# Decay attention, then a max-gated MLP, on one core: a planner with other costs and slack, and unsplit float32 products with the values in the second batch

## The chip, the core and the metric

The kernel runs on one core of a Trainium2 chip as a single program. The metric is the device time in microseconds (us) of one execution. The kernel before has a median of 991.08 us over 3 runs (990.32 to 992.14).

## The reference, cut to what matters

There are 8 batches of 8 heads, with 576 positions and 64 features per head. Everything is float32, except that the four weight matrices arrive as float64.

```python
scores = q @ k.T / 8                       # (8, 8, 576, 576)
cum = cumsum(log(clip(f, 1e-4, 1)))        # decay, per head
scores = where(causal, -1e9, scores + cum[:, None] - cum[None, :])
attn = exp(scores - rowmax); attn /= attn.sum(-1) + 1e-9
x = (attn @ v)  ->  (4608, 512)            # heads side by side
h = max(x @ w1, x @ w2, x @ w3)            # (4608, 768)
out = h @ w_out                            # (4608, 512)
```

## The kernel before, in words

**Halved operands.** Where TensorE (PE) is to work at its quick float32r format, an operand X is split into a rounded half Xh and a remainder Xl, and a product is taken as Xh·Y_h + Xh·Y_l + Xl·Y_h, three matmuls into one PSUM bank. ScalarE (ACT) writes the rounded half and VectorE (DVE) subtracts to get the remainder. The first batch (8 heads, `n < H * NB32`) isn't split: its scores and its products with the values are plain float32 matmuls, one instruction for each block.

**The attention of one head** is done as keys on the partitions and queries along the columns, in two units: unit 1 has queries 256 to 575 (five key blocks, 1,216 columns in all), unit 2 has queries 0 to 255 (two blocks, 384 columns). In the first batch unit 1 is cut into "a" and "b". `scores` (L577) makes these steps for each unit:

- a first pass on PE (`pass_a`, L606) into the score banks `s`, and the causal mask (on PE at L622 for the first two batches, on DVE at L635 and L640 after that);
- the maximum over the key blocks into `mx` (ACT L671, DVE L659, L661, L664), over the partitions into `gm` (`partition_all_reduce` on GpSimd, POOL, L674), and a copy of one row of it into the row of the query operand that shifts the scores (POOL L681, into `qs_r`);
- a second pass on PE (`pass_b`, L606 again) that adds the decay, the remainders and the shift to the same bank;
- the exponential on ACT (L688) from the bank into `pf`;
- from the second batch on, the split of `pf` into `ph` (ACT, L694) and `pl` (DVE, L695).

`values` (L698) then takes the products with the values at L709, into the bank `t`: float32 `pf` with float32 `vn` in the first batch, and three split products (`ph`·`va`, `ph`·`vl`, `pl`·`va`, put together by `split_values`, L754) after it. A column of ones in the values gives the row sums. ACT copies `t` out (L763 to L768); `finish_pair` sends the sums through DRAM, inverts and multiplies them (L778).

**Loads.** `load_quad` (L482) loads q and k of four heads, which DVE transposes (L491) and, from the second batch on, splits (ACT L495, DVE L497) into `hl`. `load_head` (L527) copies a head from `hl` into `qs_r` and `ks_r` (seven DMAs at L533). `load_v` (L501) loads the values of a pair of heads, and splits them into `va` and `vl` from the second batch on (ACT L517, DVE L518). `load_weights` (L442) loads the 24 weight pieces (L336), turns them from float64 into float32 on ACT and DVE (L468 to L474) and splits them (L477, L478). All DMAs are issued from one queue, SP.

**The MLP** of a batch (`moe`, L861) is two chunks of columns times six feature blocks of split products at L818, with the maximum on ACT and DVE (L825, L827) and a split of it (L830, L832), then products with `w_out` at L847. It runs one batch behind the attention, mixed with it.

**What sets the order.** Nothing in the code above is issued when it is written. `Plan.add` (L63) records each step with its engine, a cost in ns, a priority and the names that it reads and writes. `Plan.emit` (L82) then runs a model of the five engines: a step is ready when all that it depends on has ended, plus a lag for the pair of engines (L56). An engine that is free takes the ready step of the lowest rank, and the steps are issued in the order of their beginnings in the model. PE's clock in the model is that of `GatedClock` (L24): half speed, or full speed after a span of 3,413 ns that was busy enough. On the chip each engine works through its own fixed list, and a step that isn't ready holds up all that stand behind it on its engine.

## Time and profile before

| | |
|---|---|
| median of 3 runs | 991.08 us |
| the profiled execution's own time | 992.66 us |
| its span, first to last instruction | 990.9 us |
| PE busy | 947.8 us (96%) |
| DVE busy | 678.9 us (69%) |
| ACT busy | 513.0 us (52%) |
| POOL busy | 278.7 us (28%) |
| mean granted PE clock | 0.986 |

A busy share is the time in which an engine had an instruction under way, whatever the clock. The granted clock is given as a share of full speed. Matmuls overlap in the profile (each is recorded for about as long as it takes to pass through), so the sum of their durations is more than the time that they hold the engine. What one costs in a row of matmuls is read from the distance between starts. A wait is given as the idle time of an engine just before an instruction, with the instruction of another engine that ended it. Line numbers are those of the kernel before. In the changed kernel L336 is L353, L533 is L563, L606 is L642, L674 is L710, L681 is L717, L709 is L746, L818 is L861 and L847 is L890.

### The profile page before, as it was taken

Reading aid. Unit: us, or ns where it says so; the run is one execution under the profiler, and the core shown is the slowest. Engines: PE = TensorE matmul, PEld = TensorE weight load, DVE = VectorE, ACT = ScalarE, POOL = GpSimd, SP = SyncE. Lnnn points to the kernel's source line nnn. Section 1 sums busy time; section 2 is a strip of 40 time slices with the busy share of each in tenths; the row PEclk is TensorE's granted clock in tenths of the full one; section 3 lists DMA queues with packets and bytes.
Section 4 is the critical chain, followed back from the end, with each engine's and each line's share of the span. In section 5 each row is a group of like instructions: output and inputs, shape, how many; then the busy total and the mean of one; then the engine's idle time right before and its main releaser. Section 6 shows DMA issues by size and latency. Waiting matters only on the chain.

```text
span 990.9 us, 18561 instructions
## 1 busy us (share of the span) xinstructions
PE 947.8 (96%) x6694; PEld 879.9 (89%) x6694; DVE 678.9 (69%) x1355; ACT 513.0 (52%) x1066; POOL 278.7 (28%) x314
## 2 busy tenths in 40 slices
PE   7999897999999999999999999999999999999998
PEld 4789786998989989899999989898998989899998
DVE  8789898687776785758757686667767686543211
ACT  3476556666555564546545654546555564433111
POOL 5553305233232323233213232323232323210000
PEclk9799799999999999999999999999999999999999
DMA  7882664645444452526354343435445352400000
GB/s 208 197 232 46 169 182 97 179 102 162 111 130 118 106 149 70 152 59 165 90 155 119 92 135 84 135 82 156 108 97 152 81 141 67 119 13 35 1 32 22
DMA packets 97258, 112.69 MB, mean 114 GB/s; under 512 B 54048, under 2 KB 63520, under 8 KB 97168
## 3 DMA queue, kind: packets, MB, share of 16 engines
q1 hardware_dynamic: 97168, 111.52, 42.9%
q8 instruction: 53, 0.87, 0.4%
q14 instruction: 37, 0.30, 0.1%
HBM read 50.15 MB, written 9.86 MB: 61 GB/s over the span
## 4 chain that ended last, share of the span: by engine, by line
PE 64%; DVE 14%; POOL 10%; DMA 5%; issue 4%; SPq 2%; ACT 1%; POOLq 0%; DVEq 0%; ACTq 0%
PE mp L818 35%; PE s L606 10%; PE mp L847 9%; PE t L709 8%; POOL gm L674 6%; DVE mx L664 4%; POOL qs_r L681 3%; DVE hl L491 2%; DMA hl<-in_k_dram 2%; DVE pl_r L695 2%; SPq L533 1%; DMA ks_r<-hl 1%; DVE tm L827 1%; DVE s L635 1%; PE mp L606 1%
## 5 line engine op out<-in xcount | busy, mean ns | idle before, releaser
L818 PE MATMUL mp<-xh_r,w_r 128*128 128x320 f32 (+1 forms) x2160 | 462.7, 297 | 0.6 <-DVE tm L827 0.6
L818 PEld LDWEIGHTS mp<-xh_r,w_r 128*128 128x128 f32 x2160 | 356.7, 188 | 2.5 <-DVE tm L827 1.6
L674 POOL PARTITION_ALL_REDUCE gm<-mx x131 | 172.9, 1323 | 579.2 <-DVE mx L664 363.2
L818 PE MATMUL mp<-xl_r,w_r 128*128 128x320 f32 (+1 forms) x1080 | 319.5, 296 | 0.0
L818 PEld LDWEIGHTS mp<-xl_r,w_r 128*128 128x128 f32 x1080 | 203.2, 188 | 0.3
L827 DVE TENSOR_TENSOR tm<-mp,tm 128x256 f32<-128x256 f32 (+1 forms) x192 | 87.1, 454 | 154.0 <-PE mp L818 131.2
L688 ACT ACTIVATE pf<-s 128x384 f32<-128x384 f32 (+4 forms) x251 | 113.7, 505 | 99.8 <-PE s L606 85.3
L606 PE MATMUL s<-qs_r,ks_r 128*128 128x320 f32 (+4 forms) x784 | 132.5, 290 | 24.9 <-POOL qs_r L681 18.8
L606 PEld LDWEIGHTS s<-qs_r,ks_r 128*128 128x128 f32 (+1 forms) x784 | 114.7, 182 | 44.0 <-POOL qs_r L681 32.2
L695 DVE TENSOR_TENSOR pl_r<-pf,ph_r 128x1216 fp32r<-128x1216 f32 (+1 forms) x112 | 113.1, 1011 | 23.7 <-ACT ph_r L694 23.1
L847 PE MATMUL mp<-w_r,hmh_r 128*128 128x512 f32 (+1 forms) x396 | 123.0, 392 | 0.7 <-DVE w_r L478 0.7
L694 ACT ACTIVATE ph_r<-pf 128x1216 fp32r<-128x1216 f32 (+1 forms) x112 | 97.5, 873 | 24.3 <-PE t L709 23.2
L830 ACT ACTIVATE hmh_r<-tm 128x256 fp32r<-128x256 f32 x96 | 39.8, 415 | 129.0 <-DVE tm L827 129.0
L664 DVE TENSOR_TENSOR mx<-mx,s 128x320 f32<-128x320 f32 (+3 forms) x248 | 92.1, 371 | 9.1 <-ACT mx L671 1.9
L491 DVE STREAM_TRANSPOSE hl<-hl 128x576 f32<-128x576 f32 x64 | 75.7, 1245 | 12.5 <-DMA hl<-in_k_dram 12.5
L847 PEld LDWEIGHTS mp<-w_r,hmh_r 128*128 128x128 f32 x396 | 71.0, 189 | 13.0 <-DVE w_r L478 1.0
L681 POOL CAST qs_r<-gm 1x320 fp32r<-1x320 f32 (+1 forms) x112 | 75.2, 674 | 6.9
L847 PE MATMUL mp<-w_r,hml_r 128*128 128x512 f32 (+1 forms) x198 | 77.1, 389 | 0.0
L709 PE MATMUL t<-ph_r,va_r 128*65 128x64 f32 x392 | 61.8, 274 | 2.4 <-ACT r_r L768 1.9
L709 PE MATMUL t<-pl_r,va_r 128*65 128x64 f32 x392 | 61.3, 272 | 1.6 <-DVE pl_r L695 1.3
L709 PE MATMUL t<-ph_r,vl_r 128*65 128x64 f32 x392 | 61.6, 273 | 0.0
L825 ACT ACTIVATE tm<-mp 128x256 f32<-128x256 f32 (+1 forms) x96 | 39.4, 410 | 42.0 <-PE mp L818 40.3
(186 smaller groups left out, 1150.3 us busy)
## 6 DMA issues: line engine op xcount, KB each, us to landing
qs_r<-hl SPq DMA_DIRECT2D x168, 144.0 KB
ks_r<-hl SPq DMA_DIRECT2D x168, 144.0 KB
hl<-in_q_dram SPq DMA_DIRECT2D x16, 576.0 KB
hl<-in_k_dram SPq DMA_DIRECT2D x16, 576.0 KB
w<-in_moe_w_dram SPq DMA_DIRECT2D x18, 512.0 KB
out_dram<-o_r SPq DMA_DIRECT2D x35, 256.0 KB
r_r<-rdram SPq DMA_DIRECT2D x56, 144.0 KB
vn<-in_v_dram SPq DMA_DIRECT2D x58, 128.0 KB
```

Source lines behind the costliest of these rows:

```text
L491: add("DVE", 669, lambda e=e, tt=tt, xs=xs: nc.vector.transpose(tt[:, e], xs[:, e]), [key + "0"], [key + "1"], prio)
L606: nc.tensor.matmul(bank[bk][0:l.shape[-1], col:col + w], l, rhs(qa, w), start=start and bk not in begun, stop=stop, skip_group_check=True)
L664: nc.vector.tensor_tensor(mt[:, a:a + w], mt[:, a:a + w], bank[bk][:, col:col + w], op=ALU.max)
L674: add("POOL", 185 + 3.43 * nq, lambda: nc.gpsimd.partition_all_reduce(gm, mt, P, bass.bass_isa.ReduceOp.max), [km, km + "a"], [kg], prio)
L681: add("POOL", 100 + 0.83 * nq, lambda: nc.gpsimd.tensor_copy(shift_row(), gm[row:row + 1, :]), [kg], [kx], prio)
L688: add("ACT", act_cost(w), lambda bk=bk, w=w, col=col: nc.scalar.activation(pf[:, col:col + w], bank[bk][:, 0:w], AF.Exp, scale=sc), [kb[bk ...
L694: add("ACT", act_cost(PW[unit]) + 40, lambda: nc.scalar.activation(ph(unit), pf, AF.Copy), [fk], [hk], prio)
L695: add("DVE", dve_cost(PW[unit]), lambda: nc.vector.tensor_tensor(pl(unit), pf, ph(unit).bitcast(F32), op=ALU.subtract), [fk, hk], [lk], prio)
L709: nc.tensor.matmul(t[:D + 1, qa:qa + w], src()[:, j, c, :], pr()[:, col:col + w], start=first and x == 0, stop=last, skip_group_check=True,)
L818: nc.tensor.matmul(m, unit_w(i, fb)[:, w, kt, :], xx, start=kt == 0 and x == 0, stop=kt == KT - 1 and x == 2,)
L827: add("DVE", dve_cost(cn), lambda m=m: nc.vector.tensor_tensor(t, m, t, op=ALU.max), [km, kt_], [kt_], prio)
L847: nc.tensor.matmul(mp[:, 0:cn], l[:, fb, cs], unit_o(fb)[:, r, ds], start=fb == 0 and x == 0, stop=fb == FT - 1 and x == 2,)
```

## The change

There are two parts.

**The planner's numbers.** `emit` now gives each step more time than its cost on all engines but PE and SP (`ROOM`: 30 ns on ACT and DVE, 450 ns on POOL), takes 5% off PE's, and lets a DMA land 400 ns later (`LATE`). A matmul's cost per column goes from 0.4167 ns (1/2.4) to 0.4477 ns, and a number of single costs are set anew (the transposes at L491 from 669 to 1,085 ns, the decay's steps, memsets, small copies, the all-reduce). The modelled clock goes to full speed at a share of 0.72 of a span (0.65 before) and stays there above 0.34 (0.4). The 20 warm-up matmuls at the start go to the bank `SP1[0]`; before, they went to `MPS[2]`, which the first transposes use too. The memsets of the key rows come later in DVE's ranks.

**The second batch's products with the values.** For heads 8 to 15 (`H * NB32 <= n < NV32`, with `NV32 = 2 * H`) the values are loaded as float32 straight into `va0` and `va1` (L531 and L534 of the changed kernel), and `scores` ends after the exponential. `values` multiplies them in one go, as float32 matmuls. The exponentials of odd heads go to a second float32 buffer, made of the space of `ph1` and `ph2` (`pg`), so that two heads have one each. The split, with its constants, begins at head 16.

```diff
-        self.warm = share > (0.4 if self.warm else 0.65)
+        self.warm = share > (0.34 if self.warm else 0.72)
...
+    ROOM = {"PE": (0.95, 0), "ACT": (1.0, 30), "DVE": (1.0, 30), "POOL": (1.0, 450), "SP": (1.0, 0)}
+    LATE = 400
...
-            end = t + self.steps[i][1]
+            cost = self.steps[i][1] * self.ROOM[e][0] + self.ROOM[e][1]
+            end = t + cost
             if e == "PE":
-                end = clock.run(t, self.steps[i][1], self.steps[i][6])
+                end = clock.run(t, cost, self.steps[i][6])
             free[e] = end
             done += 1
             if self.steps[i][5]:
-                end = moved = max(moved, end + 650) + self.steps[i][5]
+                moved = max(moved, end + 650) + self.steps[i][5]
+                end = moved + self.LATE
...
 def mm_cost(cols, m):
-    return max(cols / 2.4 + 3, 107 if m > 65 else 55)
+    return max(0.4477 * cols + 3, 107 if m > 65 else 55)
...
+    NV32 = 2 * H
...
+    def VF(i):
+        return lazy(f"va{i}", [P, 2, 5, D + 1], F32, "f")
...
+    def pg(u):
+        return lazy(f"ph{u}", [P, PW[u]], F32, "f")
...
+    def second_constants():
+        for i in range(2):
+            nc.gpsimd.memset(VF(i)[64:P, :, 4, :], 0.0)
+            nc.gpsimd.memset(VF(i)[:, :, :, D:D + 1], 1.0)
...
-            add("PE", 217, lambda: nc.tensor.matmul(MPS[2].rearrange("p (o x) -> p o x", o=4), ident, z, start=True, stop=True),
-                ["const"], ["mp2"], 90)
+            add("PE", 217, lambda: nc.tensor.matmul(SP1[0].rearrange("p (o x) -> p o x", o=4), ident, z, start=True, stop=True),
+                ["const"], ["sp1/0"], 90)
...
-                add("DVE", 669, lambda e=e, tt=tt, xs=xs: nc.vector.transpose(tt[:, e], xs[:, e]),
+                add("DVE", 1085, lambda e=e, tt=tt, xs=xs: nc.vector.transpose(tt[:, e], xs[:, e]),
...
+        if NB32 * NP <= pi < NV32 // 2:
+            for j in range(2):
+                add("SP", 475, lambda j=j: nc.sync.dma_start(
+                    out=VF(s)[:, j, 0:4, 0:D], in_=src[j, 0:512, :].rearrange("(c p) d -> p c d", p=P)),
+                    [], [f"va{s}/{j}"], prio, 262144 / 360)
+            add("SP", 475, lambda: nc.sync.dma_start(
+                out=VF(s)[0:64, :, 4, 0:D], in_=src[:, 512:S, :].rearrange("h p d -> p h d")), [], [f"va{s}/2"], prio, 300000 / 360)
+            return
...
-        add("POOL", 185 + 3.43 * nq, lambda: nc.gpsimd.partition_all_reduce(
+        add("POOL", 450 + 2.6 * nq, lambda: nc.gpsimd.partition_all_reduce(
...
+        pk = f"ph{unit}" if H * NB32 <= n < NV32 and n % 2 else None
...
-        if first:
+        if n < NV32:
             return
         fk, hk, lk = f"pf{unit}", f"ph{unit}", f"pl{unit}"
...
-        split_values(s, unit, av, ca, kt, hk, lk, prio)
+        if n < NV32:
+            odd = n % 2
+            pr = lambda: pg(unit) if odd else PF[unit]
+            add("PE", sum(4.04 * x[2] / 2.4 for x in cols),
+                lambda: av(lambda: VF(s), pr, True, True), [hk if odd else f"pf{unit}", f"va{s}"], [kt], prio)
+        else:
+            split_values(s, unit, av, ca, kt, hk, lk, prio)
...
-    add("POOL", 200, split_constants, w=["va0", "va1", "vl"], prio=p)
+    add("POOL", 1200, second_constants, w=["va0", "va1"], prio=p)
...
+        if n == NV32:
+            add("POOL", 1000, split_constants, w=["va0", "va1", "vl"], prio=p)
```

The program's lists change nearly everywhere. Three places are shown, each as it stood and as it stands; in each, the names are tiles of the program (numbers at their ends count buffers).

POOL, late in the program, where attention and MLP run mixed: `gm_84` is the all-reduce of unit 1, `gm_85` that of unit 2, and the CAST behind each copies the row that releases the second pass. Before:

```order
L674 ISA gm_85<-mx_83 128x256
L681 CAST qs_r<-gm_85 1x256
L674 ISA gm_84<-mx_82 128x320
L681 CAST qs_r<-gm_84 1x320
L674 ISA gm_84<-mx_82 128x320
```

Now:

```order
L710 ISA gm_84<-mx_82 128x320
L710 ISA gm_85<-mx_83 128x256
L717 CAST qs_r<-gm_84 1x320
L717 CAST qs_r<-gm_85 1x256
L710 ISA gm_84<-mx_82 128x320
```

The all-reduce of unit 2 has moved in between the all-reduce of unit 1 and its copy. Such a pair stood 4 times in the list, and stands there 32 times now.

PE, in the second batch: the products of one unit 1 with the values, into the bank `t`. Before:

```order
L709 MATMUL t<-ph_r,va_r 65x64
L709 MATMUL t<-ph_r,va_r 65x192
L709 MATMUL t<-ph_r,va_r 65x320 x3
L709 MATMUL t<-ph_r,vl_r 65x64
L709 MATMUL t<-ph_r,vl_r 65x192
L709 MATMUL t<-ph_r,vl_r 65x320 x3
L709 MATMUL t<-pl_r,va_r 65x64
L709 MATMUL t<-pl_r,va_r 65x192
L709 MATMUL t<-pl_r,va_r 65x320 x3
```

Now, with the MLP's products ahead and the next scores behind:

```order
L890 MATMUL mp_128<-w_r,hmh_r 128x512 x2
L890 MATMUL mp_128<-w_r,hml_r 128x512
L746 MATMUL t<-ph_f,va_f 65x64
L746 MATMUL t<-ph_f,va_f 65x192
L746 MATMUL t<-ph_f,va_f 65x320 x3
L642 MATMUL s_126<-qs_r,ks_r 128x256
L642 MATMUL s_126<-qs_r,ks_r 128x128
```

Fifteen split matmuls have become five in float32.

SP, where the second batch's first heads are loaded: `w9` and up are weight pieces; `qs0`, `ks0` are head 8's operands and `qs1`, `ks1` head 9's. Before:

```order
L336 DMA w9_104<-in_moe_w1_dram 128x4x256
L533 DMA ks1_r_616<-cdram_131 2x576
L336 DMA w10_105<-in_moe_w2_dram 128x4x256
L336 DMA w11_106<-in_moe_w3_dram 128x4x256
L336 DMA w12_107<-in_moe_w1_dram 128x4x256
L336 DMA w13_108<-in_moe_w2_dram 128x4x256
L336 DMA w14_109<-in_moe_w3_dram 128x4x256
L533 DMA qs0_r_486<-hl_73 32x1152
L533 DMA qs1_r_618<-hl_73 32x1152
L533 DMA qs0_r_486<-hl_73 32x2x576
L533 DMA ks0_r_484<-hl_73 32x2x576
```

Now:

```order
L353 DMA w9_104<-in_moe_w1_dram 128x4x256
L563 DMA ks0_r_607<-cdram_131 2x576
L563 DMA qs0_r_609<-hl_73 32x1152
L353 DMA w10_105<-in_moe_w2_dram 128x4x256
L563 DMA ks0_r_607<-hl_73 32x2x576
L353 DMA w11_106<-in_moe_w3_dram 128x4x256
L563 DMA ks0_r_607<-hl_73 32x2x576
L563 DMA qs0_r_609<-hl_73 32x2x576 x2
L563 DMA qs1_r_679<-hl_73 32x2x576
L563 DMA ks1_r_677<-hl_73 32x2x576
L563 DMA qs1_r_679<-hl_73 32x2x576
L563 DMA ks1_r_677<-hl_73 32x2x576
```

Head 8's and head 9's copies have moved ahead of the pieces `w12` to `w14`, and head 8's begin ahead of `w10`.

More of the change, by code (lines that the diff above doesn't have):

```diff
@@ L136, in mm_cost @@
 def mm_cost(cols, m):
-    return max(cols / 2.4 + 3, 107 if m > 65 else 55)
+    return max(0.4477 * cols + 3, 107 if m > 65 else 55)
 def run_cost(cols):
     load = [m / 1.2 for _, m in cols[1:]] + [107]
-    return sum(max(n / 2.4 + 3, x) for (n, _), x in zip(cols, load))
+    return sum(max(0.4477 * n + 3, x) for (n, _), x in zip(cols, load))
 def act_cost(cols):
@@ L198 @@
         plan.parts[f"vn{i}"] = [f"vn{i}/{x}" for x in range(3)]
+    for i in range(2):
+        plan.parts[f"va{i}"] = [f"va{i}/{x}" for x in range(3)]
     plan.parts["r"] = ["r/0", "r/1"]
@@ L208 @@
     plan.parts["pf1"] = [f"pf1/{x}" for x in range(3)]
+    plan.parts["ph1"] = [f"ph1/{x}" for x in range(3)]
+    plan.parts["ph2"] = ["ph2/0"]
     for c in ("mx", "gm", "sg"):
@@ L365, in split_constants @@
         nc.gpsimd.memset(VL()[:, :, :, D:D + 1].bitcast(F32), 0.0)
+    def second_constants():
+        for i in range(2):
+            nc.gpsimd.memset(VF(i)[64:P, :, 4, :], 0.0)
+            nc.gpsimd.memset(VF(i)[:, :, :, D:D + 1], 1.0)
     def sums_constants():
@@ L376 @@
     add("POOL", 2500, sums_constants, w=[f"rs{g}{u}" for g in range(2) for u in (1, 2)] + ["sel"], prio=0.0)
-    add("POOL", 1800, constants, w=["const"], prio=-9)
-    add("POOL", 150, lambda: nc.gpsimd.memset(LESS.bitcast(F32), -1.0), w=["less"], prio=-9)
+    add("POOL", 1100, constants, w=["const"], prio=-9)
+    add("POOL", 200, lambda: nc.gpsimd.memset(LESS.bitcast(F32), -1.0), w=["less"], prio=-9)
     for i in range(H):
-        add("POOL", 480, lambda i=i: first_constants(i), w=[f"qf{i}/2"], prio=-9 + i)
-        add("DVE", 369, lambda i=i: nc.vector.memset(KF[i][64:P, :], 0.0), w=[f"kf{i}/2"], prio=-9 + i)
-    add("POOL", 1000, value_constants, w=[f"vn{i}" for i in range(4)], prio=-8)
+        add("POOL", 525, lambda i=i: first_constants(i), w=[f"qf{i}/2"], prio=-9 + i)
+        add("DVE", 605, lambda i=i: nc.vector.memset(KF[i][64:P, :], 0.0), w=[f"kf{i}/2"], prio=-5.5 + 0.1 * i)
+    add("POOL", 1650, value_constants, w=[f"vn{i}" for i in range(4)], prio=-8)
     def decay():
@@ L574, in buffers @@
     def buffers(n, unit):
-        return SETS[n % len(SETS) if n < H * NB32 else 0] if unit == 2 else BUFS[unit]
+        if n < H * NB32:
+            return SETS[n % len(SETS)] if unit == 2 else BUFS[unit]
+        bufs = SETS[0] if unit == 2 else BUFS[unit]
+        if n < NV32 and n % 2:
+            bufs = bufs[:3] + (None,) + bufs[4:]
+        return bufs
     def scores(n, unit, prio):
@@ L646, in scores @@
             cost[run] = run_cost(ws)
-            ca = sum(4 * w / 2.4 for w, _ in ws) if first else cost[run]
+            ca = sum(4.04 * w / 2.4 for w, _ in ws) if first else cost[run]
             ca += 65 * mask_pe * sum(x[0] in run for x in diag)
@@ L666, in scores @@
         by_act = n < 0 if unit == 2 else True
-        cm = sum(dve_cost(x[1] * x[4]) for x in d["first"] if not (x[4] == 1 and by_act)) + sum(
+        cm = sum(dve_cost(x[1] * x[4]) + 110 * (x[4] == 3) for x in d["first"] if not (x[4] == 1 and by_act)) + sum(
             dve_cost(x[1]) + 128 for x in d["more"]) - 128 * (by_act and bool(d["more"]))
@@ L688, in scores @@
             add("ACT", act_cost(w), lambda bk=bk, w=w, col=col: nc.scalar.activation(
-                pf[:, col:col + w], bank[bk][:, 0:w], AF.Exp, scale=sc),
-                [kb[bk]], PFKEYS.get((unit, bk), [f"pf{name}"]), prio)
-        if first:
+                (pg(unit) if pk else pf)[:, col:col + w], bank[bk][:, 0:w], AF.Exp, scale=sc),
+                [kb[bk]], [f"{pk}/{bk}"] if pk else PFKEYS.get((unit, bk), [f"pf{name}"]), prio)
+        if n < NV32:
             return
```

26 lines of the change are left out of this document (13 added, 13 removed).

## The prediction

> **What bounds the kernel now.** I read the page first, then the stages, then what PE waits for in each stage.
>
> ```profile
> span 990.9 us, 18561 instructions
> PE 947.8 (96%) x6694; PEld 879.9 (89%) x6694; DVE 678.9 (69%) x1355; ACT 513.0 (52%) x1066; POOL 278.7 (28%) x314
> ```
>
> PE is the bound on average. What a new order can give is PE's idle time, 990.9 - 947.8 = 43.1 us, and the time lost at a lower clock. The busy time by stages (us, then PE's granted clock) says where these are:
>
> ```profile
> 0.00:100.00 100.00, 90.66 (x601) 76.90 (x602) 87.86 (x161) 55.92 (x122) 49.55 (x88) 0.93 0.65 171
> 100.00:200.00 100.00, 89.22 (x625) 81.00 (x624) 83.69 (x154) 61.34 (x123) 29.05 (x30) 0.93 0.57 153
> 200.00:900.00 700.00, 680.43 (x4895) 639.63 (x4894) 486.18 (x993) 378.55 (x780) 200.15 (x196) 1.00 0.43 112
> 900.00:990.90 90.90, 87.49 (x582) 82.38 (x580) 21.23 (x51) 17.22 (x43) 0.00 (x0) 1.00 0.06 23
> ```
>
> The columns after the length are PE, PEld, DVE, ACT and POOL. PE is idle for 9.3 us in the first stage (first batch, weights), 10.8 in the second (the second batch's attention, mostly), 19.6 from 200 to 900, 3.4 in the tail. A clock of 0.93 over 100 us is worth some 7 us in each of the first two. There DVE, at 84 to 88%, is nearly as full as PE. After 200 it isn't, and one wait makes nearly all of PE's idle time:
>
> ```profile
> PE s L606 <- POOL qs_r L681: 17.3, 31, 1.4
> PE s L606 <- DMA qs_r<-hl: 0.7, 1, 0.7
> PE s L606 <- DMA ks_r<-hl: 0.4, 1, 0.4
> PE s L606 <- issue: 0.3, 1, 0.3
> PE t L709 <- DVE pl_r L695: 0.2, 1, 0.2
> ```
>
> This is PE's list of waits from 200 us to the end (total, times, longest): second passes that were issued before their row of maxima was there. By shape, over the whole program:
>
> ```profile
> L606 PE MATMUL s<-qs_r,ks_r 128*128 128x320 f32 x336 | 94.6, 350 | 14.4 <-POOL qs_r L681 8.5 <-issue 2.4 <-ACT pf L688 2.0
> L606 PE MATMUL s<-qs_r,ks_r 128*128 128x256 f32 x112 | 34.6, 309 | 10.5 <-POOL qs_r L681 10.3
> ```
>
> So 8.5 us of it is unit 1's (320 columns), 10.3 us unit 2's; 1.5 of these 18.8 us lie before 200.
>
> **Term A, the steady waits on POOL.** The old planner put the second pass too near; the new one gives POOL 450 ns more for each of two steps. Counted in the lists over 56 heads, the matmuls between a unit's first pass and its second go from a median of 47 to 59.5 in unit 1, and from 37 to 61 in unit 2. What a matmul of the MLP with 256 columns holds PE for is the distance between starts:
>
> ```profile
> 614.77 0.40 PE L818 MATMUL mp<-xh_r,w_r 128*128 128x256 f32 x2
> 617.26 0.27 PE L818 MATMUL mp<-xh_r,w_r 128*128 128x256 f32 x1
> ```
>
> Between these stand 21 matmuls in 2.49 us, 119 ns each. Unit 2 gains 24 x 0.119 = 2.9 us of distance, twice its longest wait; its 10.3 us go. Unit 1 gains 12.5 x 0.119 = 1.5 us, but in the pairs that the POOL list now has, its copy stands behind one more all-reduce:
>
> ```profile
> L674 POOL PARTITION_ALL_REDUCE gm<-mx x131 | 172.9, 1323 | 579.2 <-DVE mx L664 363.2
> ```
>
> At 1.3 us for that, unit 1 nets 0.2 us, well below its longest wait. I credit half of its 8.5. Less 0.6 for the part before 200 us (it is in B), A = -(10.3 + 4.3 - 0.6) = **-14**. Its bounds are -17.3 (all gone) and -8 (unit 1 not helped, and unit 2 in part held up by the same pairs).
>
> **Term B, the second batch.** Each head there loses two roundings and two subtractions, each pair of heads a split of the values:
>
> ```profile
> L695 DVE TENSOR_TENSOR pl_r<-pf,ph_r 128x1216 fp32r<-128x1216 f32 (+1 forms) x112 | 113.1, 1011 | 23.7 <-ACT ph_r L694 23.1
> L694 ACT ACTIVATE ph_r<-pf 128x1216 fp32r<-128x1216 f32 (+1 forms) x112 | 97.5, 873 | 24.3 <-PE t L709 23.2
> ```
>
> DVE sheds 16 x 1.01 = 16 us and ACT 16 x 0.87 = 14 us, mostly between 100 and 200, where DVE was busy for 83.7. PE's waits there were these:
>
> ```profile
> PE s L606 <- issue: 2.2, 1, 2.2
> PE s L606 <- ACT pf L688: 2.0, 2, 1.2
> PE t L709 <- ACT r_r L768: 1.9, 1, 1.9
> PE s L606 <- POOL qs_r L681: 1.5, 3, 0.8
> PE t L709 <- DVE pl_r L695: 1.1, 2, 0.7
> ```
>
> The DVE and ACT rows are what the relief is for. The row "issue" is a late load, as SP's queue shows:
>
> ```profile
> 63.35 3.58 SPq L336 DMA_DIRECT2D w<-in_moe_w_dram  x5
> 91.32 3.23 SPq L533 DMA_DIRECT2D qs_r<-hl  x3
> 105.74 0.65 PE L606 MATMUL s<-qs_r,ks_r 128*128 128x320 f32 x4 [2.15 <-issue]
> ```
>
> SP issued nothing between 67 and 91 us: head 8's and 9's operands stood behind a transposed and split `hl` that DVE had put late, and all came at once. In the new lists DVE's first split of `hl` (L497) stands ahead of weight piece `w_105`, where it stood behind `w_107`, and SP issues the copies among the weights, as the third pair of lists shows. The clock fell with such waits:
>
> ```profile
> 115.00:120.00 5.00, 3.20 (x17) 2.57 (x18) 5.00 (x12) 3.93 (x9) 2.11 (x2) 0.68 0.81 196
> 120.00:125.00 5.00, 5.00 (x31) 4.92 (x30) 4.90 (x11) 2.33 (x5) 1.99 (x2) 0.64 0.90 249
> 165.00:170.00 5.00, 3.21 (x24) 2.14 (x22) 3.36 (x6) 3.68 (x7) 0.77 (x3) 1.00 0.82 192
> 170.00:175.00 5.00, 4.29 (x19) 3.69 (x19) 3.38 (x5) 3.02 (x7) 2.17 (x2) 0.66 0.23 52
> ```
>
> Twice PE was busy for 3.2 of 5 us, with no single wait over 2.2, and 5 us at 0.64 to 0.66 came behind (the first of these stretches was at 0.68 already). The Trainium skill ("TensorE: Matmul & The Clock Gate", section "HAM oscillation") warns only of PE-idle gaps over about 3.4 us. By that alone these falls of the clock would have another cause and stay, which leaves B about 4 us smaller. This trace differs: the clock fell after a run of short waits. I take 7 of the 10.8 idle us and 4 of the 7 us of clock: B = **-11**, with bounds of -18 (all of both) and -4 (the late load and DVE's rows alone).
>
> **Term C, the first batch.** The first 100 us have 9.3 us idle and 7 of clock. The largest waits:
>
> ```profile
> PE s L606 <- POOL ph L681: 2.0, 2, 1.9
> PE mp L432 <- DMA hml<-in_k_dram: 1.6, 2, 1.1
> PE mp L417 <- POOL ident masks.py:199: 1.5, 1, 1.5
> ```
>
> With the warm-up in another bank the transposes of head 0 needn't wait for the last of it, SP issues head 1's raw q and k ahead of the decay's rows, and the maxima of two heads go through POOL together; the wait for `ident` stays. But DVE, at 88%, has the same work to do. C = **-4**, between -8 and +2, since a longer run of single-row second passes could also cost clock.
>
> **Term D, float32 products.** In the split form a unit 1 takes three passes, and a unit 2 three:
>
> ```profile
> 617.54 0.75 PE L709 MATMUL t<-ph_r,va_r 128*65 128x64 f32 x5
> 618.13 0.75 PE L709 MATMUL t<-ph_r,vl_r 128*65 128x64 f32 x5
> ...
> 622.19 0.34 PE L709 MATMUL t<-ph_r,va_r 128*65 128x128 f32 x2
> 622.37 0.34 PE L709 MATMUL t<-ph_r,vl_r 128*65 128x128 f32 x2
> ```
>
> From start to start a pass is 0.59 us and 0.18 us, so a head is 3 x 0.77 = 2.3 us. The float32 form is in the first batch (two records to a block; these ten are 704 columns):
>
> ```profile
> 79.68 1.37 PE L709 MATMUL t<-pf,vl 128*65 128x64 f32 x10
> 80.88 0.60 PE L739 MATMUL mp<-ph,hdl 97*128 97x256 f32 x2
> ```
>
> They take 1.20 us, 1.7 ns a column; 1,600 columns are 2.7 us. The change costs PE 0.4 to 0.45 us a head, 8 heads: D = **+3.6**. The Trainium skill speaks against the change more sharply ("FP8 and Floating Point Precision", section "TensorE Precision Notes"): true float32 is four passes through the array; four in place of three would be a third of 2.3 us, 6 us in all, an estimate. The row is lower, since the split's small blocks don't run at the full column rate; the sum goes by the row. D lies between 0, where it fills time in which PE would have waited, and +5.5, at the clock of 0.66 of the rows above.
>
> **Term E, new waits.** Where values followed unit 1's second pass after a median of 113 matmuls, they now follow after 28 (3.3 us at 119 ns). The next head's first pass follows the second within 17 matmuls in 40 of 55 cases, where it was 20. In between lie three exponentials on ACT, and for the values the rounding too. Of the old 20, those after 200 us made no row in the list of waits; in the second batch such rows made 2.0 us on the exponentials and 1.1 on `pl_r`, on a DVE that was full. I take **+4** (0.1 us on each close pass), between 0 and +12.
>
> **The sum.** -14 - 11 - 4 + 3.6 + 4 = -21.4. The profiled execution took 992.66 us, 1.6 over the median of 991.08; 992.7 - 21.4 = 971.3 there, and 969.7, so **970 us**, as a median. The tail of 3.4 us and all other MLP work stay.
>
> **Rivals.**
> - *Close passes on a busy ACT and DVE (slower).* If what stands close now waits as the second batch's did, with 2.0 + 1.9 + 1.1 = 5.0 us over 8 heads, that is 0.6 us a head, over 56 heads 35 us in place of 4: 970 + 31 = 1001. It takes the whole gain from (21.4 + 4) / 56 = 0.45 us a head on. Against it: after 200 us DVE is busy for 69% and these rows come to 0.2 us in all. Chance 0.09.
> - *The pairs on POOL.* The copy of unit 1 waits for two all-reduces, and the second of these for DVE's maxima of unit 2; the wait on POOL changes its place and A is worth 4. 970 + 10 = 980. For it: 32 such pairs. Against it: the planner's own times gave POOL 0.9 us more. Chance 0.12.
> - *The second batch stays.* Weights and loads, not DVE, hold that stage, and the clock isn't won back: B is 0. 970 + 11 = 981. For it: DMA busy 57% there. The rule on gaps that the Trainium skill has (term B) leads here too. Chance 0.14.
> - *All of it goes.* A, B and C at their ends, E at 0: 992.7 - 17.3 - 18 - 8 + 3.6 = 953, 951 as a median. Chance 0.07.
> - The forecast itself, 962 to 977: 0.58.
>
> **The numbers.** 0.2% of 991 us, 2 us, is about what a measurement of this kernel can tell from no change. Faster by more: 0.58 + 0.12 + 0.14 + 0.07, 0.91, less 0.01 for the tails of the two at 980; no change 0.03 and slower 0.07, both from the first rival and those tails. The range takes in the forecast and both rivals near 980 with their spread of 4 us, and stops short of 951 and of 1001: 958 to 985.
>
> **What would show it.** Right: PE's waits on `qs_r` after 200 us down from 17.3 to 3 or so; PE idle after 200 us under 10 us (19.6 + 3.4 before); DVE's busy time lower by 16 us or more; the SP queue without the gap from 67 to 91 us; granted clock from 100 to 200 us at 0.97 or more; float32 values at 2.7 us a head. Wrong: rows of PE waiting for `pf`, `ph_r` or `pl_r` that come to over 12 us; waits on POOL that stay near 17; a granted clock that is still 0.93 in the second stage.

## The result, and the profile after

The changed kernel takes 959.23 us, the median of 4 runs (957.70 to 960.07), beside 990.70 us for the kernel before in 4 runs on the same chip. The ratio is 0.9683, with a 95% interval of 0.9660 to 0.9706. So the kernel became 31.5 us faster where 21 were forecast. 959.2 lies in the range, at its lower end, and 3 us below the forecast case's own 962 to 977. The profiled execution took 959.11 us.

The page's head, and the stages at the prediction's cuts (length, then PE, PEld, DVE, ACT, POOL, then PE's clock):

```profile
span 957.2 us, 18214 instructions
PE 932.9 (97%) x6638; PEld 874.2 (91%) x6638; DVE 658.8 (69%) x1335; ACT 489.6 (51%) x1046; POOL 244.9 (26%) x318
```

```profile
0.00:100.00 100.00, 84.63 (x541) 72.29 (x542) 86.86 (x154) 51.61 (x112) 49.21 (x85) 0.88 0.72 183
100.00:200.00 100.00, 96.18 (x681) 86.42 (x682) 78.25 (x155) 55.27 (x123) 29.41 (x39) 1.00 0.55 147
200.00:900.00 700.00, 698.27 (x5047) 665.14 (x5046) 482.78 (x1002) 373.30 (x789) 166.28 (x194) 1.00 0.44 112
900.00:957.20 57.20, 53.85 (x374) 50.39 (x372) 10.92 (x26) 9.47 (x23) 0.00 (x0) 1.00 0.07 24
```

The first stage is worse than before (PE idle for 15.4 us instead of 9.3, clock 0.88 instead of 0.93), the second better (3.8 instead of 10.8, clock 1.00 instead of 0.93), and from 200 to 900 us 1.7 us of idle time are left of 19.6. Nothing has taken the place of the waits on POOL. This is all that PE waits for after 200 us that is long enough to be listed:

```profile
PE mp L861 <- ACT tm L868: 0.7, 2, 0.5
PE s L642 <- issue: 0.6, 2, 0.4
PE mp L861 <- DVE tm L870: 0.2, 1, 0.2
PE t L746 <- ACT u L806: 0.2, 1, 0.2
```

**Where the 33.7 us of span come from.** ACT's last copy of a row of sums marks the end of a batch's attention. In the kernel before, the second batch's last and the eighth batch's last are

```profile
217.69 0.38 ACT L768 ACTIVATE r_r<-t 1x256 f32<-1x256 f32 x1
891.57 0.38 ACT L768 ACTIVATE r_r<-t 1x256 f32<-1x256 f32 x1 [0.96 <-PE t L709]
```

and in the changed kernel

```profile
209.78 0.38 ACT L811 ACTIVATE r_r<-t 1x256 f32<-1x256 f32 x1
858.36 0.38 ACT L811 ACTIVATE r_r<-t 1x256 f32<-1x256 f32 x1
```

So the program falls into a **start** (to the end of the second batch), 217.7 us before and 209.8 after, a **steady part** of six batches, 891.57 - 217.69 = 673.9 and 858.36 - 209.78 = 648.6, and the rest, 99.3 and 98.8 (each counted from the beginning of such a row). The start gave 7.9 us, the steady part 25.3.

**Idle time understates the waits.** The steady part gave more than the 17.9 us of idle time that it lost. A few rows of PE in the kernel before show why (start, length, instruction):

```profile
637.28 0.46 PE L818 MATMUL mp<-xh_r,w_r 128*128 128x320 f32 x2
637.58 0.31 PE L818 MATMUL mp<-xl_r,w_r 128*128 128x320 f32 x1
637.72 0.31 PE L818 MATMUL mp<-xh_r,w_r 128*128 128x320 f32 x1
639.41 0.91 PE L606 MATMUL s<-qs_r,ks_r 128*128 128x320 f32 x5 [1.38 <-POOL qs_r L681]
```

Such matmuls start 0.14 to 0.15 us apart, but each is recorded for 0.31 us. The one at 637.72 would have had its successor at 637.87; it came at 639.41, 1.54 us late, and the row says 1.38. A wait behind such a product is listed 0.16 us short, and one under 0.16 us doesn't show at all: it counts as busy. For the score products after 200 us, all shapes in one row, before and after:

```profile
L606 PE MATMUL s<-qs_r,ks_r 128*128 128x320 f32 (+4 forms) x679 | 112.6, 288 | 19.2 <-POOL qs_r L681 17.3 <-DMA qs_r<-hl 0.7 <-DMA ks_r<-hl 0.4
```

```profile
L642 PE MATMUL s<-qs_r,ks_r 128*128 128x320 f32 (+4 forms) x672 | 101.5, 280 | 0.6 <-issue 0.6
```

Busy and idle together they go from 131.8 to 102.1 us, 29.7 less for 7 products fewer, where the idle column alone gives 18.6. From the starts of all matmuls of the trace, each distance less the median of its shape, I get the same: PE waited 34 us at the scores after 200 us, and waits 5 now. Over the steady part, all products together, PE's waits of whatever length go by this count from 44 to 17 us, while the time that the products themselves hold PE stays as it was (630 and 632 us). Below, "busy plus idle at the scores" is this sum of the row after 200 us.

### The profile page after: what moved, and what is told of

It is laid out like the page before. It is cut to its first block, busy times and chain, and to the rows that moved or that the text cites. A ratio compares the mean times of both kernels' runs of the same rounds, so it can differ in the third digit from the quotient of the medians.

```text
span 957.2 us, 18214 instructions
## 1 busy us (share of the span) xinstructions
PE 932.9 (97%) x6638; PEld 874.2 (91%) x6638; DVE 658.8 (69%) x1335; ACT 489.6 (51%) x1046; POOL 244.9 (26%) x318
## 4 chain that ended last, share of the span: by engine, by line
PE 86%; DMA 3%; DVE 1%; SPq 1%; issue 0%; ACT 0%; DVEq 0%; ACTq 0%
PE mp L861 45%; PE mp L890 16%; PE t L746 14%; PE s L642 10%; DMA w<-in_moe_w_out_dram 1%; SPq L563 1%; DMA qs_r<-hl 1%; DMA rdram<-sc 1%; DMA r_r<-rdram 0%; PE s L658 0%; DVE ph L778 0%; DVE mx L700 0%; PE t L782 0%; SPq L353 0%; DVE tm L870 0%
## 5 line engine op out<-in xcount | busy, mean ns | idle before, releaser
L861 PE MATMUL mp<-xh_r,w_r 128*128 128x320 f32 (+1 forms) x2160 | 472.8, 298 | 0.9 <-ACT tm L868 0.7
L861 PEld LDWEIGHTS mp<-xh_r,w_r 128*128 128x128 f32 x2160 | 359.3, 188 | 4.6 <-ACT tm L868 1.3
L861 PE MATMUL mp<-xl_r,w_r 128*128 128x320 f32 (+1 forms) x1080 | 319.4, 296 | 0.0
L710 POOL PARTITION_ALL_REDUCE gm<-mx x131 | 158.0, 1224 | 575.2 <-DVE mx L700 449.8
L861 PEld LDWEIGHTS mp<-xl_r,w_r 128*128 128x128 f32 x1080 | 203.4, 188 | 0.8
L725 ACT ACTIVATE pf<-s 128x384 f32<-128x384 f32 (+2 forms) x235 | 103.6, 507 | 60.6 <-PE s L642 58.1
L642 PE MATMUL s<-qs_r,ks_r 128*128 128x320 f32 (+4 forms) x784 | 122.0, 282 | 2.2 <-DMA w<-in_moe_w_out_dram 1.6
L732 DVE TENSOR_TENSOR pl_r<-pf,ph_r 128x1216 fp32r<-128x1216 f32 (+1 forms) x96 | 96.4, 1012 | 6.9 <-ACT ph_r L731 6.7
L513 DVE STREAM_TRANSPOSE hl<-hl 128x576 f32<-128x576 f32 x64 | 76.4, 1245 | 13.6 <-DMA hl<-in_k_dram 7.4
L731 ACT ACTIVATE ph_r<-pf 128x1216 fp32r<-128x1216 f32 (+1 forms) x96 | 83.3, 883 | 2.0 <-PE t L746 1.4
L890 PEld LDWEIGHTS mp<-w_r,hmh_r 128*128 128x128 f32 x396 | 69.4, 188 | 10.8
L676 DVE TENSOR_TENSOR s<-s,mask 128x64 f32<-128x64 f32 x48 | 11.1, 231 | 73.7 <-PE s L642 73.6
L875 DVE TENSOR_TENSOR hml_r<-tm,hmh_r 128x256 fp32r<-128x256 f32 x96 | 43.8, 456 | 19.9 <-ACT hmh_r L873 19.2
L717 POOL CAST qs_r<-gm 1x320 fp32r<-1x320 f32 (+1 forms) x112 | 54.5, 502 | 5.1
L746 PE MATMUL t<-ph_r,va_r 128*65 128x320 f32 (+4 forms) x336 | 52.2, 271 | 0.2 <-ACT u L806 0.2
```

Of the source, the lines that this page charges most:

```text
L513: add("DVE", 1085, lambda e=e, tt=tt, xs=xs: nc.vector.transpose(tt[:, e], xs[:, e]), [key + "0"], [key + "1"], prio)
L642: nc.tensor.matmul(bank[bk][0:l.shape[-1], col:col + w], l, rhs(qa, w), start=start and bk not in begun, stop=stop, skip_group_check=True)
L710: add("POOL", 450 + 2.6 * nq, lambda: nc.gpsimd.partition_all_reduce(gm, mt, P, bass.bass_isa.ReduceOp.max), [km, km + "a"], [kg], prio)
L717: add("POOL", 130 + 0.9 * nq, lambda: nc.gpsimd.tensor_copy(shift_row(), gm[row:row + 1, :]), [kg], [kx], prio)
L725: add("ACT", act_cost(w), lambda bk=bk, w=w, col=col: nc.scalar.activation((pg(unit) if pk else pf)[:, col:col + w], bank[bk][:, 0:w], AF. ...
L731: add("ACT", act_cost(PW[unit]) + 40, lambda: nc.scalar.activation(ph(unit), pf, AF.Copy), [fk], [hk], prio)
```

## Experiments

The theory: the planner's new numbers, above all the room for POOL's steps, take the waits off the second passes, and that is most of the gain. The first rival: the float32 sums free DVE and ACT, and that is the gain. All runs together; the start and the steady part (us) are read from the one profiled execution of each. The kernel before was run again beside the other kernels, with medians of 992.3 to 993.6 us, and each ratio is to those runs: medians of different rows can be up to 3 us apart for that reason, so where it matters the ratios are compared.

| kernel | median | ratio to before, 95% | start | steady |
|---|---|---|---|---|
| before | 990.70 | 1 | 218 | 674 |
| changed | 959.23 | 0.966 to 0.971 | 210 | 649 |
| planner's numbers only | 961.26 | 0.963 to 0.973 | 215 | 649 |
| float32 sums only | 989.61 | 0.994 to 0.998 | 218 | 671 |
| changed, no room for POOL | 978.11 | 0.979 to 0.991 | 214 | 662 |
| before, with POOL's room only | 980.29 | 0.981 to 0.989 | 229 | 652 |
| changed, 225 ns for POOL | 959.27 | 0.963 to 0.971 | 211 | 648 |
| changed, 900 ns for POOL | 997.10 | 1.002 to 1.007 | 235 | 669 |
| changed, no other room | 964.48 | 0.968 to 0.975 | 209 | 650 |
| changed, all old costs | 950.96 | 0.955 to 0.961 | 206 | 647 |
| changed, weights behind heads | 961.91 | 0.964 to 0.973 | 212 | 650 |
| changed, old costs at the start | 964.36 | 0.967 to 0.974 | 212 | 649 |
| changed, third batch float32 | 958.37 | 0.961 to 0.967 | 209 | 647 |
| changed, all batches float32 | 972.84 | 0.978 to 0.984 | 209 | 664 |

The rest, behind the steady part, takes 99 us in all but two: 95 with the planner's numbers only, 89 with 900 ns for POOL.

### The two parts alone

The planner's numbers without the float32 batch:

```diff
-    NV32 = 2 * H
+    NV32 = H
...
-    add("POOL", 1200, second_constants, w=["va0", "va1"], prio=p)
```

> The changed kernel with the planner's new numbers, but the second batch's value sums on halves as before. Theory 1 (the planner's room takes away the waits on the second passes, and that is most of the gain; the float32 sums give the rest, by freeing VectorE and ScalarE while TensorE waits for them): about 969 us, 22 under the kernel before and 10 over the changed one, with under 3 us of TensorE waits on the shift's row after 200 us and 8 to 11 us idle between 100 and 200 us. Rival (the relief in the second batch is the gain, since it lets the whole later program run ahead of its buffers): 980 us or more, with the shift's row waited for as in the kernel before.

It took 961.26 us, ratio 0.9677 (0.9629 to 0.9725), not to be told from the changed kernel's 0.9683. The second stage of this kernel:

```profile
100.00:200.00 100.00, 94.92 (x707) 88.48 (x707) 87.98 (x166) 64.43 (x134) 32.29 (x35) 0.97 0.51 140
```

DVE has its splits back (88.0 us of 100, 78.3 in the changed kernel), and yet PE is idle for only 5.1 us and the clock is 0.97. So in time the planner gives the whole gain, more than either theory had said. The parts differ: this kernel's start is 5 us longer than the changed kernel's (214.8 and 209.8), which the float32 batch does shorten, and its rest is 3.5 us shorter (95.4 and 98.9). Why the rest is shorter isn't shown.

The float32 batch alone has the planner's numbers of before (room 0, old costs and thresholds):

```diff
-    ROOM = {"PE": (0.95, 0), "ACT": (1.0, 30), "DVE": (1.0, 30), "POOL": (1.0, 450), "SP": (1.0, 0)}
-    LATE = 400
+    ROOM = {"PE": (1.0, 0), "ACT": (1.0, 0), "DVE": (1.0, 0), "POOL": (1.0, 0), "SP": (1.0, 0)}
+    LATE = 0
```

> The kernel before with its old planner numbers, and the second batch's value sums as float32 products alone. Theory 1: about 981 us, 10 under the kernel before; 15 us or more of waits on the shift's row stay after 200 us. Rival (relief is the gain): 970 us or less. The gains of this run and of the run with the planner alone should add to 31 us if the parts don't help each other.

989.61 us, ratio 0.9961 (0.9937 to 0.9984): 4 us (2 to 6), less than both had said. Its waits after 200 us begin with

```profile
PE s L642 <- POOL qs_r L717: 15.3, 28, 1.3
```

so they stayed, as the theory had it. Relief for DVE and ACT by itself is worth little: the rival falls. The gains of the two runs, 32 and 4 us, add to 36 where both together gave 31.5; beside the planner's numbers the float32 batch adds nothing to the time that these runs can tell.

### How much room POOL's steps need

```diff
-    ROOM = {"PE": (0.95, 0), "ACT": (1.0, 30), "DVE": (1.0, 30), "POOL": (1.0, 450), "SP": (1.0, 0)}
+    ROOM = {"PE": (0.95, 0), "ACT": (1.0, 30), "DVE": (1.0, 30), "POOL": (1.0, 0), "SP": (1.0, 0)}
```

> The changed kernel, where the planner gives GpSimd's steps no 450 ns more (every other new number stays). Theory 1 in its narrow form (this one number moves the second passes away from their rows): 959 + 14 to 17 = 973 to 976 us, and waits on the shift's row return after 200 us, 10 us or more. Rival (the new costs, the room for DMA landings or the clock's thresholds do it together): 959 to 963 us, with under 5 us of such waits.

978.11 us, 19 more than the changed kernel (17 by the ratios, 0.9854 and 0.9683), so at or just above the 973 to 976 of the theory, and the waits are back:

```profile
PE s L642 <- POOL qs_r L717: 9.6, 19, 0.8
```

```profile
L642 PE MATMUL s<-qs_r,ks_r 128*128 128x320 f32 (+4 forms) x674 | 108.2, 286 | 10.4 <-POOL qs_r L717 9.6 <-DMA r_r<-rdram 0.3 <-issue 0.3
```

Busy plus idle at the scores is 118.6 us, half of the way back to 131.8, and the steady part is 13 us longer. With the new costs, this one number still makes half of the steady gain. The kernel before with this number alone:

```diff
-            end = t + self.steps[i][1]
+            end = t + self.steps[i][1] + (450 if e == "POOL" else 0)
```

> The kernel before, where the planner gives each GpSimd step 450 ns more, and nothing else is changed. Theory 1 in its narrow form: the 34 us that the scores wait after 200 us (by the spacing of the products' starts) fall to under 15, and the time is 991 - 17 = 974 us (970 to 978). Rival (the room works only with the planner's other numbers, since its old costs for TensorE run the plan ahead of the chip): over 982 us.

980.29 us, above the expected 970 to 978 but under the rival's 982; by the ratio (0.9852 of 990.7) it would be 976. By the starts of its products PE waits 12 us at the scores after 200 us, as the theory had it (under 15). Its steady part is 652 us, 22 of the 25 us gained: with the old costs the room alone nearly suffices there. The other half, which the run above kept without it, may come from the new costs of POOL's own steps. In the kernel before, the copy of the row took

```profile
L681 POOL CAST qs_r<-gm 1x320 fp32r<-1x320 f32 x56 | 38.1, 680 | 3.6
L681 POOL CAST qs_r<-gm 1x256 fp32r<-1x256 f32 x56 | 37.4, 667 | 3.3
```

0.68 and 0.67 us where the old costs (100 + 0.83 ns a column) gave it 0.37 and 0.31; the new ones give 0.42 and 0.36. So the planner lacked some 0.3 us on each copy, and the new costs bring 0.05 of it and the room the rest and more. Which of the new costs made that half was not tried alone, and it stays open.

But the start of this kernel became 11 us longer (229 us), with PE idle for 13.7 us here:

```profile
100.00:200.00 100.00, 86.33 (x614) 79.13 (x613) 78.36 (x146) 55.47 (x116) 30.33 (x33) 0.95 0.52 135
```

Half of the room, and double:

```diff
-    ROOM = {"PE": (0.95, 0), "ACT": (1.0, 30), "DVE": (1.0, 30), "POOL": (1.0, 450), "SP": (1.0, 0)}
+    ROOM = {"PE": (0.95, 0), "ACT": (1.0, 30), "DVE": (1.0, 30), "POOL": (1.0, 225), "SP": (1.0, 0)}
```

> The changed kernel with 225 ns in place of 450 for each GpSimd step. If each ns short of the real lag costs the same, halfway between none (978) and 450 (959): 966 to 971 us, with the scores waiting some 12 us after 200 us by the spacing of the products. If the lag that is missing from the planner's numbers is about 225 ns: 958 to 962 us. If the room is worth having only whole: 975 us or more.

959.27 us, as with 450, and the scores' waits are gone with 225 already (the list after 200 us has one of 0.2 us on `qs_r`). The missing time is at most 225 ns a step, given the new costs.

A rival stands in POOL's own rows. In the changed kernel the copies of the row are shorter than before:

```profile
L717 POOL CAST qs_r<-gm 1x320 fp32r<-1x320 f32 x56 | 29.1, 519 | 3.5
L717 POOL CAST qs_r<-gm 1x256 fp32r<-1x256 f32 x56 | 27.2, 485 | 1.7
```

Without the room they take 0.68 and 0.67 us again, with 225 ns 0.57 and 0.56. Did the quicker copies end the waits? The time from the end of each copy to the start of its second pass says no. Behind the second batch, in the kernel before, unit 2's second passes begin 0.05 us after their copy at the nearest, and half of them within 0.41 us. In the changed kernel unit 1's begin at least 1.09 us after it (median 2.05), and unit 2's at least 0.45 us (median 2.36). With copies slower by 0.16 to 0.18 us none of them would wait: it is the distance in the lists that ended the waits.

Now 900 ns:

```diff
-    ROOM = {"PE": (0.95, 0), "ACT": (1.0, 30), "DVE": (1.0, 30), "POOL": (1.0, 450), "SP": (1.0, 0)}
+    ROOM = {"PE": (0.95, 0), "ACT": (1.0, 30), "DVE": (1.0, 30), "POOL": (1.0, 900), "SP": (1.0, 0)}
```

> The changed kernel with 900 ns in place of 450 for each GpSimd step. Theory 1 (with 450 the scores hardly wait any more, so that there is nothing left to gain): 958 to 961 us. Rival A (more room moves still shorter waits): 953 to 956 us. Rival B (the room holds score banks longer and leaves the planner too few): over 963 us.

997.10 us, slower than the kernel before. The waits after 200 us have changed their owners:

```profile
PE t L746 <- DVE pl_r L732: 4.6, 5, 1.4
PE mp L861 <- DVE tm L870: 2.4, 2, 1.2
PE t L746 <- ACT u L806: 2.3, 3, 1.6
PE t L746 <- ACT ph_r L731: 2.2, 4, 0.7
```

No row waits for POOL any more; the value products wait for the split and for the copies out of their bank instead, and the MLP's products for the maximum. By the starts PE waits 14 us at the value products and 20 at L861 after 200 us, where the changed kernel has 0.5 and 11. The size of rival B came true, but that score banks were the reason isn't shown: no row names one. With too much room the plan is wrong at another place, and the start, at 235 us, loses more than the steady part. The prediction's rival of close passes is seen here in part: the rows on `pf`, `ph_r` and `pl_r` come to 8.6 of the 18 us that are listed.

### The other numbers of the planner

Without the room for DMA landings and the 30 ns on ACT and DVE:

```diff
-    ROOM = {"PE": (0.95, 0), "ACT": (1.0, 30), "DVE": (1.0, 30), "POOL": (1.0, 450), "SP": (1.0, 0)}
-    LATE = 400
+    ROOM = {"PE": (0.95, 0), "ACT": (1.0, 0), "DVE": (1.0, 0), "POOL": (1.0, 450), "SP": (1.0, 0)}
+    LATE = 0
```

> The changed kernel without the 400 ns that the planner adds to each landing of a DMA and without the 30 ns on VectorE's and ScalarE's steps; GpSimd's 450 ns and the new costs stay. If the new costs, with GpSimd's room, carry what that room alone didn't (the kernel before with the room alone took 980 us): 957 to 963 us. If the room for landings and the 30 ns carry it: 970 us or more, with the second batch ending near 225 us.

964.48 us, ratio 0.9711 (0.9676 to 0.9746): 1.5 us above the expected 957 to 963, with an interval that overlaps the changed kernel's. The start is as short as with them (209 us, in a profiled execution that was the fastest of its four, 959.92 us). That seemed to leave the new costs as the source of the short start. The changed kernel with all the old costs (and the old bank of the warm-up and rank of the key rows' memsets, and without the 5% off PE's), its other rooms and its thresholds kept; four places of the edit:

```diff
-    ROOM = {"PE": (0.95, 0), "ACT": (1.0, 30), "DVE": (1.0, 30), "POOL": (1.0, 450), "SP": (1.0, 0)}
+    ROOM = {"PE": (1.0, 0), "ACT": (1.0, 30), "DVE": (1.0, 30), "POOL": (1.0, 450), "SP": (1.0, 0)}
...
-    return max(0.4477 * cols + 3, 107 if m > 65 else 55)
+    return max(cols / 2.4 + 3, 107 if m > 65 else 55)
...
-        add("POOL", 450 + 2.6 * nq, lambda: nc.gpsimd.partition_all_reduce(
+        add("POOL", 185 + 3.43 * nq, lambda: nc.gpsimd.partition_all_reduce(
...
-                add("DVE", 1085, lambda e=e, tt=tt, xs=xs: nc.vector.transpose(tt[:, e], xs[:, e]),
+                add("DVE", 669, lambda e=e, tt=tt, xs=xs: nc.vector.transpose(tt[:, e], xs[:, e]),
```

> The changed kernel with all the old costs of steps (TensorE's products, VectorE, ScalarE and GpSimd) and the old bank of the warm-up; the rooms, the clock's thresholds and the float32 second batch stay. If the new costs carry what GpSimd's room alone leaves open (980 against 959 us): 972 to 980 us, with the second batch ending at 222 us or later. If the thresholds of the clock or the float32 products do: 958 to 964 us, with it ending near 210 us.

950.96 us, ratio 0.9582 (0.9553 to 0.9610), outside both expectations and the fastest of all: it beats the kernel before by 41 us and the changed one by about 10. My account of the start by the costs falls. From 100 to 200 us PE is now idle for 0.2 us:

```profile
50.00:100.00 50.00, 45.80 (x283) 41.12 (x284) 45.36 (x81) 31.61 (x70) 17.79 (x26) 0.83 0.55 150
100.00:200.00 100.00, 99.76 (x712) 90.11 (x712) 76.46 (x157) 52.78 (x121) 36.23 (x40) 1.00 0.59 157
```

Its steady part (647 us) is the changed kernel's; 4 of the 5 us by which its span is shorter lie in the start (206 us). (The profiled execution was the slowest of its four, 954.17 us, so its trace holds only half of the 10.) It differs from the kernel before with POOL's room (229 us) by the room for landings with the 30 ns, the clock's thresholds and the float32 batch. Which of these makes the 23 us of the start stays open. The costs that agree better with the chip (the transposes' 1,085 ns, say) aren't what made the gain.

### The late start

In the changed kernel head 1's transposes (L454) stand ahead of head 0's first scores and wait for raw keys:

```profile
6.96 3.20 PE L439 MATMUL s<-ident 128*128 128x512 bf16 x14
15.05 1.74 PE L454 MATMUL mp<-tm,hml 96*64 96x96 f32 x12 [4.90 <-DMA hml<-in_k_dram]
...
18.65 1.65 PE L642 MATMUL s<-qs 128*128 128x256 f32 x4
```

SP issued these keys at 6.07 us, behind two quads of q and k and three weight pieces. First scores came at 14.0 us before, and the first batch's last group of value products starts at 111.54 instead of 102.14 us. Weights put behind the heads:

```diff
-        after = [f"wh{step - PD}"] if step >= PD else []
+        after = [f"wh{step - PD}"] if step >= PD else ["rawk", "rawq"]
```

> The changed kernel, where the first three weight pieces are loaded only behind the second transfer of raw queries and keys. Theory of the late start (head 1's turns stand ahead of head 0's scores on TensorE and wait for raw keys that queue behind these weights): the 4.9 us wait at 15 us goes, the first batch's last value product moves from 113 to about 107 us, and the time is 954 to 956 us. Rival (the first stage is bound by VectorE and the clock, not by its start): 958 to 960 us. The third way (the weights are late for the first unit's products): over 961 us, with waits on the weights near the first gates.

The wait is down to 0.72 us and the first scores come at 13.0 us, as the theory said; but the time is 961.91 us, ratio 0.9684 (0.9637 to 0.9731), as good as the changed kernel's 0.9683. No product waits for a weight, so the third way isn't what happened. The first batch's last value products, expected near 107 us, start at 119.9 us, later than the changed kernel's 111.5: PE waits twice for `ks` (2.9 and 1.8 us, at 20 and 27 us) where the changed kernel waits once (3.0 us), and the lists have another order. The changed kernel's and this one's first 135 us:

```profile
0.00:135.00 135.00, 116.34 (x794) 102.16 (x795) 119.50 (x220) 71.95 (x158) 61.20 (x102) 0.91 0.67 171
```

```profile
0.00:135.00 135.00, 118.10 (x770) 101.99 (x771) 114.41 (x213) 69.87 (x154) 61.70 (x99) 0.87 0.62 166
```

PE was busier by 1.8 us, at a clock of 0.87 instead of 0.91: 135 x 0.04 = 5.4 us, about the 5.6 us of the earlier start. So much more was lost to the clock; that the earlier start brought the lower clock isn't shown, since the order and other waits changed with it. The other way, the old costs for the start's steps, which puts head 0's scores ahead of two of head 1's turns again (seven such lines, two shown; the cost of the transposes at L491 holds for all batches):

```diff
-        add("DVE", 605, lambda i=i: nc.vector.memset(KF[i][64:P, :], 0.0), w=[f"kf{i}/2"], prio=-5.5 + 0.1 * i)
+        add("DVE", 369, lambda i=i: nc.vector.memset(KF[i][64:P, :], 0.0), w=[f"kf{i}/2"], prio=-5.5 + 0.1 * i)
...
-        add("DVE", 1275, lambda: nc.vector.tensor_tensor_scan(
+        add("DVE", 669, lambda: nc.vector.tensor_tensor_scan(
```

> The changed kernel with the old costs for the steps of the start (memsets, the decay's VectorE steps, the 32x32 turns), which puts head 0's scores ahead of the last two turns of head 1 again. Theory of the late start: first scores at 14 us instead of 18.6, and 954 to 957 us. Rival (an earlier start is given back to the clock or to VectorE before the first batch ends, as when the weights were put behind the heads): 959 to 963 us.

964.36 us, ratio 0.9702 (0.9669 to 0.9735), with first scores at 15.9 us: no gain either, as the rival said, and 1 us above its 959 to 963. The late start is real, but taking it away, wholly or in part, didn't make the kernel faster in these two runs. In the run with all the old costs, too, the first scores come early, at 14.7 us, and the first batch's last value products begin less than 1 us sooner than the changed kernel's.

### The price of the float32 products

In the changed kernel, a unit 2 and then another head's unit 1, with the MLP's products behind each:

```profile
185.87 0.81 PE L746 MATMUL t<-ph_f,va_f 128*65 128x128 f32 x4
186.33 0.50 PE L861 MATMUL mp<-xh_r,w_r 128*128 128x320 f32 x1
186.67 0.31 PE L861 MATMUL mp<-xl_r,w_r 128*128 128x320 f32 x1
...
190.95 2.22 PE L746 MATMUL t<-pf,va_f 128*65 128x64 f32 x10
192.76 0.55 PE L861 MATMUL mp<-xh_r,w_r 128*128 128x320 f32 x1
193.15 0.31 PE L861 MATMUL mp<-xl_r,w_r 128*128 128x320 f32 x1
```

From their starts to the second product behind them, less 0.15 us for the first: 193.15 - 190.95 - 0.15 = 2.05 and 186.67 - 185.87 - 0.15 = 0.65, so 2.7 us a head, as forecast. (To the first product behind them it is only 1.81 + 0.46 us: the last block's second record starts 0.03 us ahead of the next product, and the time shows one product later.) The third batch in the same form:

```diff
-    NV32 = 2 * H
+    NV32 = 3 * H
```

> The changed kernel with the third batch's value sums as float32 products too. Theory (in a stage where TensorE waits for nobody, only the price of the products counts): eight heads at 2.7 instead of 2.3 us, 959 + 3 = 962 us (960.5 to 964). Rival (the relief of VectorE and ScalarE is worth more than the products cost): under 958 us.

958.37 us, ratio 0.9642 (0.9613 to 0.9672): not the 3 us more that the price alone would make, and not under 958 either; by the ratio it is 4 us under the changed kernel, with intervals that just overlap. PE is recorded as busy there without a break:

```profile
200.00:500.00 300.00, 299.82 (x2086) 280.22 (x2084) 204.37 (x436) 154.12 (x335) 81.72 (x93) 1.00 0.49 125
```

so what pays for the 3.4 us must be waits too short to be listed. The starts of PE's products tell where. The third batch itself becomes 4.1 us longer (110.1 us instead of 106.0), and its waits stay (2.6 and 2.5 us). The five batches behind it, whose products are as they were, wait for 9.7 us instead of 14.4. So the price shows where it is paid, and what pays it back lies in batches that got no relief; why they wait less isn't shown. All later batches:

```diff
-    NV32 = 2 * H
+    NV32 = 8 * H
```

> The changed kernel with the value sums of all seven later batches as float32 products. They cost 2.7 instead of 2.3 us a head by the spacing of the products, 0.42 x 48 heads = 20 us of TensorE over the changed kernel. Theory (TensorE waits for next to nothing after 200 us, so the price shows): 959 + 20 = 979 us, less at most the 5 us of short waits at the scores: 974 to 979. Rival (VectorE and ScalarE still hold TensorE up in waits too short to be listed, as the third batch hints): 950 to 958 us.

972.84 us, ratio 0.9808 (0.9780 to 0.9835): 13.6 us more than the changed kernel (12 by the ratios), of 20 by the price, and 1 us under the theory's range. In the steady part the products hold PE for 19 us more, and its waits, by the starts, fall from 17 to 13 us. So the price is real and nearly all of it shows; the 3.5 us that come back are shorter waits, of which, as in the run above, it isn't shown that the relief of DVE and ACT made them. In the second batch the whole time shows neither a gain nor a price.

## Why the prediction was right, and where not

- **The sum** was -21.4, measured -31.5. Direction, the main mechanism and the range were right, and the size was short by 10. That 959.2 lies inside the range, by 1 us, is partly luck: the steady part gave 15 us more than terms A and E together had, and the start 3.5 less than B, C and D together. With the start as forecast, the time would have been near 956, below the range.
- **Term A** (-14, bounds -17.3 and -8) is the step that failed, in its size. The waits on POOL after 200 us went from 17.3 to 0, where I had left 3 or so, and PE's idle time there fell to 5.1 us (1.7 and 3.4). But I read the size from the idle column, and "all gone" was taken as its bound. The steady part gave 25.3 us, since each listed wait is some 0.16 us too short and others aren't listed: busy plus idle at the scores fell by 29.7. The halving for unit 1, for the copies that now stand behind one more all-reduce, was also wrong: unit 1's waits went as unit 2's did, and the nearest of its second passes now stands 1.09 us behind its copy. (A small slip: the part before 200 us is 0.8 us of unit 2's waits and 0.7 of unit 1's, so 1.1 and not 0.6 should have come off.)
- **Terms B to E in the start.** I had B -11, C -4 and D +3.6, and the start gave -7.9. The parts differ. **B** was right for the stage (idle 10.8 to 3.8 us, clock 0.93 to 1.00), but its cause, the relief, holds only in part: with the planner's numbers alone the stage has 5.1 idle us and a clock of 0.97, with the relief alone 8.3 and 0.97. To the end of the second batch the planner's numbers alone gain 2.9 us, the relief alone 0.2, both 7.9. The SP queue does send the second batch's operands from 67.6 us on, as forecast, but it still has a gap, from 79.4 to 91.3 us. **C** had the wrong sign: the first 100 us have 15.4 idle us instead of 9.3, at a clock of 0.88 instead of 0.93, and the first batch's last value products start 9.4 us later, in place of 4 us gained. I had seen that head 1's raw loads move up in SP's list, and not that on PE head 1's transposes moved ahead of head 0's scores. **D** had the right price in PE's time (2.7 us a head); in the second batch the relief and the price can't be told apart.

SP's rows in the changed kernel (start, length, DMAs) around the gap named under B:

```profile
77.85 0.59 SPq L563 DMA_DIRECT2D qs_r<-hl  x1
78.54 0.39 SPq L563 DMA_DIRECT2D ks_r<-cdram  x1
78.98 0.38 SPq L353 DMA_DIRECT2D w<-in_moe_w_dram  x1
91.32 0.62 SPq L563 DMA_DIRECT2D ks_r<-hl  x1
```

- **Term E** (+4) was 0.2 us in the list of waits after 200 us: values 28 matmuls behind their second pass are far enough, with DVE at 69%.
- **The clock.** That the clock falls after a run of short waits fits the other side: with those gone, the stage from 100 to 200 us runs at 1.00. No wait there was over 2.2 us, so gaps alone, the rule in the Trainium skill ("TensorE: Matmul & The Clock Gate", section "HAM oscillation"), don't explain the falls of before. The granted clock in the records of both kernels is 1.00 or 0.50, and the prediction's 0.64 to 0.68 are means of the two over 5 us. Two falls of the kernel before, each behind the 3.4 us ahead of it:

```profile
113.40:116.80 3.40, 1.95 (x14) 1.47 (x13) 3.40 (x9) 1.67 (x4) 1.49 (x2) 1.00 0.33 76
116.80:123.60 6.80, 6.01 (x28) 5.31 (x27) 6.70 (x14) 3.97 (x7) 2.59 (x3) 0.50 0.94 240
168.00:171.40 3.40, 1.49 (x12) 1.16 (x13) 3.30 (x7) 1.13 (x4) 1.64 (x2) 1.00 0.80 181
171.40:174.80 3.40, 3.40 (x12) 2.87 (x11) 1.98 (x3) 2.56 (x6) 0.84 (x1) 0.50 0.04 9
```

All nine falls in these two traces, up to the last product, come behind 3.4 us in which PE was busy for 0.4 to 2.2. But the changed kernel has two such stretches (1.8 and 1.9 us busy, to 117.9 and 128.1 us) without a fall behind them, so the busy share alone doesn't settle it, and the rest stays open.
- **The rivals.** Pairs on POOL: no wait on POOL is left. The second batch stays: it didn't. Close passes: not at 450 ns; at 900 such rows come, with 8.6 us listed, under the 12 that the prediction named as the sign. All of it goes (951): the steady part did more than that, and the start less.
